# Second mixture-of-experts stage: where squares, high parts, output products and sums stand in a step

## The chip, the cores and the metric

One core of a Trainium2 chip. The metric is device time in microseconds (us) of one execution of the whole program, median of several. TensorE (PE) multiplies matrices, VectorE (DVE), ScalarE (ACT) and GpSimd (POOL) work elementwise, SyncE (SP) issues transfers. Each engine runs its own instructions strictly in the order in which they were issued, and waits on semaphores for the others.

## The reference

Attention over 4 batches of 8 heads and 576 positions with a decaying bias gives 2304 tokens of 512 features. Two expert layers follow, each 512 to 2048 to 512:

```python
def _moe_ref(x, w_in, w_out):
    h = np.maximum(x @ w_in, 0.0)
    return (h * h @ w_out).astype(np.float32)

def _moe2_ref(x, w_in, w_out):
    h = x @ w_in
    g = h * np.cos(h)
    return (g @ w_out).astype(np.float32)
```

## The kernel before, in words

The order is written by hand (a manual schedule): what a function issues first stands first on its engine. Attention and the first layer run woven together; this ends some 624 us into the span, and the second layer runs to the end.

**The second layer** works on five token blocks `j` (four of 512 tokens, the last of 256) and 16 feature slices `f` of 128. `GROUPS` cuts the slices into three passes `p` (4, 5 and 7 slices), and `steps2` is the list of all (p, j, f): 80 steps. In step i,

- `m2_g1` multiplies block j by slice f of the input weights: 12 matmuls on PE into `hp` (three PSUM buffers). Numbers are split into a high and a low half (`yh`, `yl`; two parts per weight), so there are three passes per 128 rows;
- `m2_cos` makes the cosine's argument `a` on ACT, rounds it on DVE in two instructions (`kf`), and takes the sine on ACT;
- `m2_mul` multiplies hp by the cosine on DVE and rounds it to `gh` (on POOL in pass 0, on ACT in passes 1 and 2);
- `m2_rest` makes the low half `gl` of the step before (DVE in passes 0 and 2, POOL in pass 1);
- `m2_g2` multiplies `gh`, `gl` of step i - 2 (`G2LAG`) by the output weights: 12 matmuls into up to four PSUM tiles `o0` to `o3`, one buffer each. After the last slice of a group they are evicted: in pass 0 `o0`, `o2` by ACT and `o1`, `o3` by DVE; later `o0`, `o2` by DVE and the others by ACT with an addition on POOL.

So a full step is 24 matmuls of 512 columns, and the next block's output products cannot start before `o0` is evicted.

**Weights** of the second layer are prepared on the way, a fraction per step (`P_BITS`; `B8_BITS` in the last block of the first layer). Each of 32 weight tiles is clipped by ACT (`w_clip`), gets its bits from DVE (`w_bits`, two instructions) and is squared by ACT with a row sum (`w_square`). `w_sums` adds the rows on PE: a matmul of one column into the PSUM tile `stat`. `w_scales` reads `stat` and computes the scale of a pair of tiles in short DVE instructions (`powers`), and `w_hi` (ACT, 16-bit high part) and `w_lo` (DVE, low part, in `w_lows`) split it. Lists hold the tiles between these stages: `wsq`, `wold`, `wsum`, `wnext`, `wrest`, `wlow`; `w_age` shifts them once a step. `w_step` issues low parts, high parts, bits and squares together, `w_ahead` the clips and loads of later tiles.

**Inputs** of the next block come from DRAM and are scaled by POOL (`yr`), rounded by ACT (`yh`) and subtracted by POOL (`yl`): `split_y`, called by `ready_y` in pass 0. At steps 1 and 5 two parts are issued, so the second `yh` waits for POOL's `yr`.

`step` is the step of attention and of the first layer; its last block prepares weights of the second layer too, with the same functions.

Of the kernel before, what the change touches and what calls it, by code (L numbers as in the profile page):

```python
# [23 lines left out]
NF = DFF // 128  # L24
# [6 lines left out]
GROUPS = ((0, 4), (4, 9), (9, 16))  # L31
RAWS = 6
NB2 = 5
LAG = (3, 5)
G2LAG = 2
# [3 lines left out]
def _weave(*chains):  # L39

    chains = [iter(c) for c in chains if c is not None]
    while chains:
        for c in list(chains):
            if next(c, c) is c:
                chains.remove(c)
# [50 lines left out]

EARLY = 16
FIRST_BITS = 4
B8_BITS = 0.7
P_BITS = 0.6  # L100
CLIP_AHEAD = 2
B0_BITS = 1.5
# [2 lines left out]
XST = 2  # L105
DR_BITS = 1
XST_TO = 20
# [6 lines left out]
def attention_moe_moe_kernel(  # L114
# [211 lines left out]
    lag1, wrest = [], []  # L326
# [357 lines left out]
    nw = [2, 0, 0]  # L684
    stq = [(wp, 3)]
# [55 lines left out]
    def w_square(j):  # L741
        m, f, a = wq[j]
        rw, st = wst[j]
        nc.scalar.activation(
            out=rw.rearrange("p c t -> p (c t)")[:, 0:512].bitcast(F32), in_=st, func=ACTF.Square,
            accum_out=sm["wss"][:, 2 * f + a:2 * f + a + 1],
        )
# [161 lines left out]
    def ready_y(j, i, n):  # L909

        todo = []
        for a in range(blocks[j][1] // BT):
            todo += [lambda a=a, c=c: split_y(j, a, c) for c in range(0, KD, 2)]
        todo += [lambda a=a: load_y(j + 1, a) for a in range(blocks[j + 1][1] // BT if j + 1 < NB2 else 0)]
        for x in range(len(todo) * i // n, len(todo) * (i + 1) // n):
            todo[x]()
# [17 lines left out]
    def moe_slot():  # L934
        part, n = slots.pop(0)
        k, f = chunks[n]
        if part == 1:
            w_need(2 * f + 1)
            g1(k, f)
            return n  # L940
        w_need(2 * f + 2)
        rests(n)
        g2(k, f)
        g2done[0] += 1
        if k == NB1 - 1 and 2 * f >= RAWS:
            w_load(2 * (NF + f))
            w_load(2 * (NF + f) + 1)
            nw[0] = max(nw[0], 2 * (NF + f + 1))
# [20 lines left out]
    def step(moe=0, bits=0, attn=True):  # L969

        i = prog[0]
        prog[0] += attn
        if attn:
            for j in stage(1, i - 2):
                emit_exp(j)
        x_high()
        if attn and job(i - 2):
            emit_turn(i - 2)
        if attn:
            heads_ahead(i, (next_, load_ext, 2))  # L980
        w_age()
        n = moe_slot() if moe else None
        if attn:
            heads_ahead(i, (nhigh, prep_high, 2))
        _weave(evacuate())
        if not attn:
            rests()
        _weave(softmax_tail(i) if attn else None, w_step(bits), v_early())
        x_low()
        rests()  # L990
        w_lows()
        if attn and job(i - 1) and jobs[i - 1][0] < EARLY:
            for j in stage(1, i - 1):
                emit_exp(j)
        act(n)
        if attn:
            heads_ahead(i, (nlow, prep_low, 2))
        if attn and job(i):
            emit_qk(i)
        w_sums()  # L1000
        for _ in range(moe - 1):
            act(moe_slot())
        w_scales()
        if attn:
            for j in stage(1, i - 1):
                emit_exp(j)
        if attn:
            for j in stage(0, i - 2):
                if jobs[j][1] == 0:
                    load_v(jobs[j][0])  # L1010
            for j in stage(3, i - LAG[0]):
                if j > i - lag(j):
                    stages[3] -= 1
                    break
                emit_pv(j)
        turn()
        w_ahead()
        v_late()
        if attn:
            heads_ahead(i, (nraw, load_raw, 4))  # L1020
        if later and prog[0] >= later[0][0]:
            later.pop(0)[1]()
# [6 lines left out]
    def w_clip_to(k):  # L1029
        while nw[1] <= min(k, wlim[0] - 1):  # L1030
            w_load_to(nw[1])
            w_clip(nw[1])
            nw[1] += 1

    def w_rest(j):
        w_hi(j)
        wlow.append(j)

    wlow, wsq, wold, wsum, wnext = [], [], [], [], []

    def w_age():
        wsum.extend(wold)
        wold[:] = wsq
        wsq.clear()

    def w_sums():
        while wsum:
            m, f, a = wq[wsum[0]]
            sum_rows(2 * f + a, (sm["wss"], 2 * f + a))
            wnext.append(wsum.pop(0))  # L1050

    def w_scales():
        while len(wnext) > 1:
            w_scale(wq[wnext[0]][1])
            wrest.extend(wnext[0:2])
            del wnext[0:2]

    def w_lows():
        while wlow:
            w_lo(wlow.pop(0))  # L1060

    def w_step(n):

        js = list(range(nw[2], min(nw[2] + n, wlim[0])))
        while wlow:
            w_lo(wlow.pop(0))
            yield
        while wrest:
            w_rest(wrest.pop(0))
        if js:  # L1070
            w_clip_to(js[-1])
            for _ in zip(*[w_bits(j) for j in js]):
                yield
            for j in js:
                if wq[j][0] == 0:
                    wrest.append(j)
                else:
                    w_square(j)
                    wsq.append(j)
            nw[2] += len(js)  # L1080

    def w_ahead():
        if prog[0] < FIRST_BITS:
            return
        w_clip_to(nw[2] - 1 + min(CLIP_AHEAD, stq[0][1] + (XST if nw[2] + 3 < XST_TO else 0) - len(wrest) - len(wlow) - len(wsq) - len(wold) - len(wsum) - len(wnext)))
        w_load_to(nw[2] - 1 + (WAHEAD if prog[0] else 3))

    def w_stats(j):

        while nw[2] < j:  # L1090
            _weave(w_step(1))
            w_ahead()
        if any(x < j for x in wsq + wold + wsum + wnext):
            w_age()
            w_age()
            w_sums()
            w_scales()
# [17 lines left out]
    while prog[0] < unit_done(0):  # L1115
        i = prog[0]
        x = i - FIRST_BITS
# [77 lines left out]
    hd2 = {}  # L1195
# [17 lines left out]
    def m2_cos(j, f):  # L1213
        n = blocks[j][1]
        hp = hd2[j, f]
        a = p2.tile([128, n], F32, tag="a", bufs=2, name="a")
        kf = p2.tile([128, n], F32, tag="kf", bufs=2, name="kf")
        nc.scalar.activation(out=a, in_=hp, func=ACTF.Copy, scale=sm["hsc"][:, j, f:f + 1], bias=0.25)  # L1218
        nc.vector.tensor_scalar(out=kf, in0=a, scalar1=MAGIC, scalar2=None, op0=ALU.add)  # L1219
        nc.vector.scalar_tensor_tensor(  # L1220
            out=kf, in0=kf, scalar=MAGIC, in1=a, op0=ALU.subtract, op1=ALU.subtract
        )
        nc.scalar.activation(out=a, in_=kf, func=ACTF.Sin, scale=-6.2831850)  # L1223
        hd2[j, f] = (hp, a)

    def m2_mul(p, j, f):
        n = blocks[j][1]
        hp, a = hd2[j, f]
        gh = p2.tile([128, n], F16, tag="gh", bufs=3, name="gh")
        nc.vector.scalar_tensor_tensor(  # L1230
            out=a, in0=hp, scalar=sm["gsc"][:, f:f + 1], in1=a, op0=ALU.mult, op1=ALU.mult
        )
        (nc.scalar.copy if p else nc.gpsimd.tensor_copy)(gh, a)
        hd2[j, f] = (a, gh)

    def m2_rest(p, j, f):
        n = blocks[j][1]
        a, gh = hd2[j, f]
        gl = p2.tile([128, n], F16, tag="gl", bufs=3, name="gl")
        (nc.gpsimd if p == 1 else nc.vector).tensor_tensor(out=gl, in0=a, in1=gh, op=ALU.subtract)  # L1240
        hd2[j, f] = (gh, gl)
# [35 lines left out]
    for i in range(len(steps2) + G2LAG):  # L1277
        new = i < len(steps2)
        w_age()
        if new:  # L1280
            p, j, f = steps2[i]
            w_stats(2 * NF + 2 * GROUPS[p][1])
            w_need(2 * NF + 2 * f + 2)
            m2_g1(j, f)
            m2_cos(j, f)
        w_sums()
        if i == 3:
            y_sums(NB2 - 1, NB2)
        if new and p == 0 and j + 1 < NB2:
            ready_y(j + 1, f, GROUPS[0][1])  # L1290
        if 1 <= i <= len(steps2):
            m2_rest(*steps2[i - 1])
        if new:
            goal = min(4 * NF, bits0 + int((i + 1) * P_BITS))
            _weave(w_step(max(0, goal - nw[2])))
            if nw[2] < 4 * NF:
                w_ahead()
            m2_mul(p, j, f)
            w_lows()
        w_scales()  # L1300
        if i == 4:
            y_scales(NB2 - 1, NB2)
        if i >= G2LAG:
            m2_g2(*steps2[i - G2LAG])


def _lay_out(inputs):
# [44 lines left out]
```

## Time and profile before

| | |
|---|---|
| median of 3 runs | 1031.16 us (1029.96 to 1033.33) |
| the profiled execution | 1031.54 us, of it the span of its instructions 1029.6 us |
| busy in the span | PE 94%, PEld (weight load) 72%, DVE 71%, ACT 63%, POOL 17% |
| 575 to 624 us, end of the first layer | PE 45.13 of 49.00 us, ACT 36.17, DVE 28.90 |
| 624 to 762 us | PE 121.60 of 138.00, DVE 98.85, ACT 77.05, POOL 42.26 |
| 762 to 900 us | PE 134.45 of 138.00, DVE 83.18, ACT 66.99 |
| 900 to 1029.6 us | PE 124.84 of 129.60, DVE 71.41, ACT 51.75 |

The clock numbers are us from the start of the span. Matmuls overlap, so busy PE is not PE at its peak, but idle PE is time lost.

### The profile page before, as it was taken

Reading aid. Unit: us, or ns where it says so; the run is one execution under the profiler, and the core shown is the slowest. Engines: PE = TensorE matmul, PEld = TensorE weight load, DVE = VectorE, ACT = ScalarE, POOL = GpSimd, SP = SyncE. Lnnn points to the kernel's source line nnn. Section 1 sums busy time; section 2 is a strip of 40 time slices with the busy share of each in tenths; the row PEclk is TensorE's granted clock in tenths of the full one; section 3 lists DMA queues with packets and bytes.
Section 4 is the critical chain, followed back from the end, with each engine's and each line's share of the span. In section 5 each row is a group of like instructions: output and inputs, shape, how many; then the busy total and the mean of one; then the engine's idle time right before and its main releaser. Section 6 shows DMA issues by size and latency. Waiting matters only on the chain.

```text
span 1029.6 us, 20440 instructions
## 1 busy us (share of the span) xinstructions
PE 969.4 (94%) x7266; PEld 738.3 (72%) x7266; DVE 727.4 (71%) x1862; ACT 648.7 (63%) x1574; POOL 175.9 (17%) x286
## 2 busy tenths in 40 slices
PE   4999899999999999999999987898899999999998
PEld 3788898899999998999999984344444444444444
DVE  4969889878778887777984366778756665455555
ACT  3879777777777787776764676545555544344433
POOL 4000011111111111111110023443123332011000
PEclk9999999999999999999999999899999999999999
DMA  8945489757888875487894687110000000011001
GB/s 238 332 152 176 120 202 198 169 127 156 178 170 192 181 163 150 120 171 149 204 221 89 232 304 251 42 41 1 1 1 0 1 1 1 1 41 42 11 31 62
DMA packets 150150, 126.65 MB, mean 123 GB/s; under 512 B 108064, under 2 KB 125040, under 8 KB 150048
## 3 DMA queue, kind: packets, MB, share of 16 engines
q1 hardware_dynamic: 145840, 118.20, 44.5%
q0 software_dynamic: 4192, 7.14, 2.9%
q8 instruction: 57, 0.93, 0.4%
q14 instruction: 45, 0.37, 0.1%
q10 hardware_dynamic: 16, 0.01, 0.0%
HBM read 85.25 MB, written 15.81 MB: 98 GB/s over the span
## 4 chain that ended last, share of the span: by engine, by line
PE 67%; DVE 14%; ACT 9%; DMA 5%; issue 3%; POOL 1%; SPq 1%; DVEq 0%; ACTq 0%; POOLq 0%
PE hps L839 17%; PE y L868 16%; PE o L1253 13%; PE hp L1206 11%; PE qkp L491 4%; PE pvs L585 4%; DVE st L711 2%; DVE kf L1220 2%; DVE kf L1219 1%; ACT a L1218 1%; DMA rw<-in_w_dram 1%; ACT a L1223 1%; DVE a L1230 1%; DMA c_d<-one 1%; DMA raw<-in_qk_dram 1%
## 5 line engine op out<-in xcount | busy, mean ns | idle before, releaser
L839 PE MATMUL hps<-xh,wt 128*128 128x256 f32 x1152 | 239.0, 290 | 6.9 <-ACT g L850 6.8
L868 PE MATMUL y<-gh,wt 128*128 128x256 f32 x1152 | 238.0, 290 | 0.0
L839 PEld LDWEIGHTS hps<-xh,wt 128*128 128x128 f32 x1152 | 189.9, 192 | 10.8 <-ACT g L850 9.4
L868 PEld LDWEIGHTS y<-gh,wt 128*128 128x128 f32 x1152 | 189.6, 191 | 1.3
L1206 PE MATMUL hp<-yh,wt 128*128 128x512 f16 (+1 forms) x640 | 186.4, 358 | 0.1
L1253 PE MATMUL o<-wt,gh 128*128 128x512 f16 x576 | 173.8, 384 | 10.3 <-ACT wt L1268 4.9
L868 PE MATMUL y<-gl,wt 128*128 128x256 f32 x576 | 163.1, 283 | 1.6 <-DVE gl L858 1.6
L839 PE MATMUL hps<-xl,wt 128*128 128x256 f32 x576 | 163.2, 283 | 0.9 <-DVE xl L656 0.9
L1206 PEld LDWEIGHTS <-wt 128*128 128x128 f16 x960 | 93.8, 98 | 97.9 <-issue 2.7
L1219 DVE TENSOR_SCALAR kf<-a 128x512 f32<-128x512 f32 (+1 forms) x80 | 37.4, 468 | 118.8 <-ACT a L1218 118.8
L850 ACT ACTIVATE g<-hps 128x256 f32<-128x256 f32 x144 | 54.8, 380 | 105.6 <-PE hps L839 102.4
L1223 ACT ACTIVATE a<-kf 128x512 f32<-128x512 f32 (+1 forms) x80 | 47.0, 587 | 113.9 <-DVE kf L1220 113.9
L1206 PE MATMUL hp<-yl,wt 128*128 128x512 f16 (+1 forms) x320 | 114.5, 358 | 1.5 <-POOL yl L907 1.5
L1253 PE MATMUL o<-wt,gl 128*128 128x512 f16 x288 | 110.4, 383 | 2.5 <-DVE gl L1240 2.5
L868 PEld LDWEIGHTS y<-gl,wt 128*128 128x128 f32 x576 | 110.5, 192 | 2.4 <-DVE gl L858 1.8
L839 PEld LDWEIGHTS hps<-xl,wt 128*128 128x128 f32 x576 | 110.7, 192 | 1.4 <-DVE xl L656 1.1
L1253 PEld LDWEIGHTS <-gh 128*128 128x128 f16 x576 | 55.2, 98 | 74.3 <-issue 14.2
L335 POOL DMA_DIRECT2D k<-ext_d x80 | 41.0, 513 | 331.8 <-ACT g L851 101.4
L522 ACT ACTIVATE sb<-sb,nb 128x128 f32<-128x128 f32 (+8 forms) x160 | 93.7, 586 | 2.9 <-DVE nb L505 2.6
L505 DVE CUSTOM_DVE_ANT_0 sb<-qkp,mask 128x128 f32<-128x128 f32 (+8 forms) x160 | 72.7, 455 | 16.3 <-PE qkp L482 10.9
L858 DVE TENSOR_TENSOR gl<-g,gh 128x256 fp32r<-128x256 f32 x144 | 60.1, 418 | 27.2 <-ACT gh L852 17.6
L1218 ACT ACTIVATE a<-hp,hsc 128x512 f32<-128x512 f32 (+1 forms) x80 | 51.3, 641 | 41.3 <-PE hp L1206 35.7
(115 smaller groups left out, 1691.6 us busy)
## 6 DMA issues: line engine op xcount, KB each, us to landing
rw<-in_w_dram SPq DMA_DIRECT2D x64, 512.0 KB
raw<-in_qk_dram SPq DMA_DIRECT2D x32, 352.0 KB
raw<-in_qk_dram SPq DMA_DIRECT2D x16, 384.0 KB
vr<-in_v_dram POOLq DMA_DIRECT2D x16, 320.0 KB, 4.9
v_d<-vt SPq DMA_DIRECT2D x16, 320.0 KB
raw<-in_qk_dram SPq DMA_DIRECT2D x16, 320.0 KB
vb<-v_d SPq DMA_DIRECT2D x32, 160.0 KB
y_d<-yst SPq DMA_DIRECT2D x18, 256.0 KB
```

The lines of the kernel that those rows point to most:

```text
L491: nc.tensor.matmul(p[0:r, 0:cn], m[0:kk, qo:qo + r], m[0:kk, BT + c0:BT + c0 + cn], start=(kk == 128), stop=(kk == 68),)
L505: nc.vector.tensor_tensor_reduce(out=sb[0:r, c0:c0 + cn], in0=p[0:r, 0:cn], in1=mask[0:r, mo + c0:mo + c0 + cn], scale=-0.125, scalar=(3.0 ...
L522: nc.scalar.activation(out=sb[0:r, 0:w], in_=sb[0:r, 0:w], func=ACTF.Exp, scale=-1.0, bias=j["nb"], accum_out=pd[n - h % 2]["z"][0:r, ti, ...
L839: nc.tensor.matmul(hp, w[:, a, c * 128:(c + 1) * 128], (xh, xl)[e][:, c, :], start=(n == 0), stop=(n == 3 * KD - 1),)
L850: nc.scalar.activation(out=g, in_=hp, func=ACTF.Relu)
L858: nc.vector.tensor_tensor(out=gl, in0=g, in1=gh, op=ALU.subtract)
L868: nc.tensor.matmul(yps[k][d // 2][:, d % 2, :], w[:, a, d * 128:(d + 1) * 128], (gh, gl)[e], start=(f == 0 and n == 0 and d % 2 == 0), sto ...
L1206: nc.tensor.matmul(hp, w[:, a, c * 128:(c + 1) * 128], (yh, yl)[e][:, c, :], start=(m == 0), stop=(m == 3 * KD - 1),)
L1218: nc.scalar.activation(out=a, in_=hp, func=ACTF.Copy, scale=sm["hsc"][:, j, f:f + 1], bias=0.25)
L1219: nc.vector.tensor_scalar(out=kf, in0=a, scalar1=MAGIC, scalar2=None, op0=ALU.add)
L1223: nc.scalar.activation(out=a, in_=kf, func=ACTF.Sin, scale=-6.2831850)
L1253: nc.tensor.matmul(ops[j][a], (gh, gl)[e][:, a * 128:(a + 1) * 128], w[:, x, :], start=(first and m == 0), stop=(last and m == 2),)
```

## The change

Within a step of the second layer, the same instructions are issued in another order. Squares wait in a new list `wbit` and are issued, with all high parts and the `yh` roundings, between the argument and the sine (`m2_cos` is cut, the sine is `m2_sin`). Low halves and the output products with their evictions come next; low parts, bits and the multiplication follow them. `w_scales` moves to the start of a step, `w_sums` to its end (after the output products on PE), and `wold` goes. In the first layer's last block `w_scales` and `w_sums` move the same way, and squares are issued one `w_step` later. `B8_BITS` 0.75 prepares ten weight tiles there instead of nine.

```diff
-B8_BITS = 0.7
+B8_BITS = 0.75
@@ step
         w_age()
+        w_scales()
         n = moe_slot() if moe else None
...
-        w_sums()
         for _ in range(moe - 1):
             act(moe_slot())
-        w_scales()
+        w_sums()
@@
     def w_age():
-        wsum.extend(wold)
-        wold[:] = wsq
+        wsum.extend(wsq)
         wsq.clear()
+
+    def w_squares():
+        while wbit:
+            w_square(wbit[0])
+            wsq.append(wbit.pop(0))
@@ w_step
             yield
+        w_squares()
         while wrest:
             w_rest(wrest.pop(0))
...
                 else:
-                    w_square(j)
-                    wsq.append(j)
+                    wbit.append(j)
@@ the loop over steps2
         w_age()
+        w_scales()
+        if i == 5:
+            y_scales(NB2 - 1, NB2)
         if new:
             p, j, f = steps2[i]
             w_stats(2 * NF + 2 * GROUPS[p][1])
             w_need(2 * NF + 2 * f + 2)
             m2_g1(j, f)
             m2_cos(j, f)
+            w_squares()
+            while wrest:
+                w_rest(wrest.pop(0))
+            if p == 0 and j + 1 < NB2:
+                ready_y(j + 1, f, GROUPS[0][1])
+            m2_sin(j, f)
+        if 1 <= i <= len(steps2):
+            m2_rest(*steps2[i - 1])
+        if i >= G2LAG:
+            m2_g2(*steps2[i - G2LAG])
+        if new:
+            w_lows()
+            goal = min(4 * NF, bits0 + int((i + 1) * P_BITS))
+            _weave(w_step(max(0, goal - nw[2])))
+            m2_mul(p, j, f)
+            if nw[2] < 4 * NF:
+                w_ahead()
         w_sums()
         if i == 3:
             y_sums(NB2 - 1, NB2)
-        if new and p == 0 and j + 1 < NB2:
-            ready_y(j + 1, f, GROUPS[0][1])
-        if 1 <= i <= len(steps2):
-            m2_rest(*steps2[i - 1])
-        if new:
-            goal = min(4 * NF, bits0 + int((i + 1) * P_BITS))
-            _weave(w_step(max(0, goal - nw[2])))
-            if nw[2] < 4 * NF:
-                w_ahead()
-            m2_mul(p, j, f)
-            w_lows()
-        w_scales()
-        if i == 4:
-            y_scales(NB2 - 1, NB2)
-        if i >= G2LAG:
-            m2_g2(*steps2[i - G2LAG])
```

ACT in step 5, where block 0 is evicted for the first time (argument, sine, `yh`, clips, evictions, next argument), before:

```order
L1218 ACTIVATE a<-hp_10478,hsc 128x512
L1223 ACTIVATE a<-kf 128x512
L906 CAST yh<-yr 128x2x256 x2
L701 ACTIVATE st<-rw 128x512 x2
L1268 ACTIVATE wt_9805<-o_10357,osc 128x512
L1268 ACTIVATE wt_9936<-o_10359,osc 128x512
L1218 ACTIVATE a<-hp_10528,hsc 128x512
```

and of the change:

```order
L1222 ACTIVATE a<-hp_10485,hsc 128x512
L744 ACTIVATE rw,wss<-st 128x512
L906 CAST yh<-yr 128x2x256 x2
L1231 ACTIVATE a<-kf 128x512
L1276 ACTIVATE wt_9805<-o_10365,osc 128x512
L1276 ACTIVATE wt_9939<-o_10367,osc 128x512
L1222 ACTIVATE a<-hp_10535,hsc 128x512
```

A square and both `yh` now stand ahead of the sine, and no clip ahead of the evictions.

DVE in the step of pass 1 that evicts block 0 (kf rounds the argument, L1230 is the multiplication, L760 to L765 are scales, L1260 evicts), before:

```order
L1219 TENSOR_SCALAR kf<-a 128x512
L1220 SCALAR_TENSOR_TENSOR kf<-kf,a 128x512
L707 TENSOR_SCALAR st<-st 128x512
L711 SCALAR_TENSOR_TENSOR st<-rw,st 128x512
L1230 SCALAR_TENSOR_TENSOR a<-hp_11419,gsc,a 128x512
L760 TENSOR_SCALAR wsm<-stat 128x2
L761 TENSOR_SCALAR wex<-wsm 128x2
L765 TENSOR_SCALAR wsc<-wex 128x2
L1260 SCALAR_TENSOR_TENSOR wt_9805<-o_11274,osc,wt_9805 128x512
L1260 SCALAR_TENSOR_TENSOR wt_9936<-o_11276,osc,wt_9936 128x512
```

and of the change, where the multiplication is L1238 and the eviction L1268:

```order
L760 TENSOR_SCALAR wsm<-stat 128x2
L761 TENSOR_SCALAR wex<-wsm 128x2
L765 TENSOR_SCALAR wsc<-wex 128x2
L1223 TENSOR_SCALAR kf<-a 128x512
L1224 SCALAR_TENSOR_TENSOR kf<-kf,a 128x512
L1268 SCALAR_TENSOR_TENSOR wt_9805<-o_11282,osc,wt_9805 128x512
L1268 SCALAR_TENSOR_TENSOR wt_9939<-o_11284,osc,wt_9939 128x512
L735 SCALAR_TENSOR_TENSOR wt_11444<-st,wsc,wt_11444 128x512
L735 SCALAR_TENSOR_TENSOR wt_11446<-st,wsc,wt_11446 128x512
L707 TENSOR_SCALAR st<-st 128x512
L711 SCALAR_TENSOR_TENSOR st<-rw,st 128x512
L1238 SCALAR_TENSOR_TENSOR a<-hp_11426,gsc,a 128x512
```

The evictions passed the multiplication; two low parts (L735), which stood behind it, stand ahead of it.

PE in step 5 where the input products (hp) end, before:

```order
L1206 MATMUL hp_10478<-yh,wt_9936 128x512
L753 LDWEIGHTS onesb
L753 MATMUL stat<-wss,onesb 128x1
L1253 LDWEIGHTS gh
L1253 MATMUL o_10357<-wt_10208,gh 128x512
```

and of the change at the end of that step's output products:

```order
L1261 MATMUL o_10368<-wt_10169,gl 128x512
L753 LDWEIGHTS onesb
L753 MATMUL stat<-wss,onesb 128x1
L1210 LDWEIGHTS wt_10029
L1210 MATMUL hp_10535<-yh,wt_10029 128x512
```

The sum into `stat` moved behind the twelve output products.

## Rows read from the trace of the kernel before

**Rows 1.** Who PE waited for, 575 to 624 us: total us, times, longest.

```profile
PE hps L839 <- ACT g L850: 3.7, 6, 1.1
```

**Rows 2.** Who PE waited for, 624 to 900 us: total us, times, longest.

```profile
PE o L1253 <- ACT wt L1268: 4.9, 2, 2.5
PE stat L753 <- DVE wsm L760: 4.6, 2, 3.3
PE o L1253 <- DVE wt L1260: 3.5, 3, 1.9
PE o L1253 <- DVE gl L1240: 1.6, 1, 1.6
PE o L1253 <- DVE wt L1270: 1.6, 2, 1.3
PE hp L1206 <- POOL yl L907: 1.5, 2, 1.0
PE stat L753 <- DVE ysm L760: 1.2, 1, 1.2
PE stat L753 <- ACT rw L744: 0.8, 1, 0.8
```

**Rows 3.** All engines, 640 to 680 us: window, length, busy, PEclk, DMA.

```profile
640.00:680.00 40.00, 33.75 (x144) 14.34 (x143) 28.96 (x54) 21.01 (x40) 16.14 (x16) 0.91 0.15 47
```

**Rows 4.** The chain that ended last, 570 to 900 us: start, us, what.

```profile
640.30 2.14 DVE wt L735 x2
...
660.38 1.16 POOL yl L907
661.54 1.11 POOL yr L902
...
665.02 4.42 PE o L1253 x12
...
672.04 2.59 PE o L1253 x12
```

**Rows 5.** Groups on ACT, 575 to 900 us: busy us, mean ns, idle before and releaser.

```profile
L1218 ACT ACTIVATE a<-hp,hsc 128x512 f32<-128x512 f32 (+1 forms) x54 | 35.0, 647 | 24.9 <-PE hp L1206 19.3 <-PE stat L753 5.5
L1223 ACT ACTIVATE a<-kf 128x512 f32<-128x512 f32 (+1 forms) x53 | 31.5, 594 | 77.9 <-DVE kf L1220 77.9
L726 ACT ACTIVATE wt<-st,wsc 128x512 f16<-128x512 f32 x32 | 21.2, 709 | 0.0
L744 ACT ACTIVATE rw<-st 128x512 f32<-128x512 f32 x32 | 20.0, 626 | 17.5 <-DVE st L711 17.5
L701 ACT ACTIVATE st<-rw 128x512 f32<-128x512 f32 x32 | 19.7, 659 | 0.3 <-DMA yr<-y_d 0.3
L1233 ACT CAST gh<-a 128x512 f16<-128x512 f32 (+1 forms) x33 | 19.2, 581 | 15.4 <-DVE a L1230 15.4
L906 ACT CAST yh<-yr 128x512 f16<-128x512 f32 x18 | 10.9, 607 | 5.0 <-POOL yr L902 5.0
L744 ACT ACTIVATION_READ_ACCUMULATOR rw<-st 128x1 f32 x32 | 6.0, 186 | 0.0
```

**Rows 6.** Groups on DVE, 624 to 762 us, columns as above.

```profile
L1230 DVE SCALAR_TENSOR_TENSOR a<-hp,gsc,a 128x512 f32<-128x512 f32 (+1 forms) x25 | 17.6, 705 | 4.4 <-ACT a L1223 4.4
L735 DVE SCALAR_TENSOR_TENSOR wt<-st,wsc,wt 128x512 f16<-128x512 f32 x17 | 14.9, 911 | 2.9 <-ACT wt L726 2.8
L711 DVE SCALAR_TENSOR_TENSOR st<-rw,st 128x512 int32<-128x512 int32 x16 | 11.1, 693 | 0.5
L707 DVE TENSOR_SCALAR st<-st 128x512 int32<-128x512 int32 x16 | 6.7, 420 | 0.0
```

**Rows 7.** Single instructions in order of time: start, us, engine, instruction, idle before.

```profile
623.51 0.74 DVE L735 SCALAR_TENSOR_TENSOR wt<-st,wsc,wt 128x512 f16<-128x512 f32 x1
...
623.62 0.63 ACT L744 ACTIVATE rw<-st 128x512 f32<-128x512 f32 x1 [1.40 <-DVE st L711]
...
635.86 0.39 PE L1253 MATMUL o<-wt,gl 128*128 128x512 f16 x1
```

More of the change, by code (lines that the diff above doesn't have):

```diff
@@ L1037, in w_rest @@
         wlow.append(j)
-    wlow, wsq, wold, wsum, wnext = [], [], [], [], []
+    wlow, wbit, wsq, wsum, wnext = [], [], [], [], []
     def w_age():
-        wsum.extend(wold)
-        wold[:] = wsq
+        wsum.extend(wsq)
         wsq.clear()
+    def w_squares():
+        while wbit:
+            w_square(wbit[0])
+            wsq.append(wbit.pop(0))
     def w_sums():
@@ L1084, in w_ahead @@
             return
-        w_clip_to(nw[2] - 1 + min(CLIP_AHEAD, stq[0][1] + (XST if nw[2] + 3 < XST_TO else 0) - len(wrest) - len(wlow) - len(wsq) - len(wold) - len(wsum) - len(wnext)))
+        w_clip_to(nw[2] - 1 + min(CLIP_AHEAD, stq[0][1] + (XST if nw[2] + 3 < XST_TO else 0) - len(wrest) - len(wlow) - len(wbit) - len(wsq) - len(wsum) - len(wnext)))
         w_load_to(nw[2] - 1 + (WAHEAD if prog[0] else 3))
@@ L1092, in w_stats @@
             w_ahead()
-        if any(x < j for x in wsq + wold + wsum + wnext):
-            w_age()
+        if any(x < j for x in wbit + wsq + wsum + wnext):
+            w_squares()
             w_age()
@@ L1222, in m2_cos, with m2_sin @@
         )
+        hd2[j, f] = (hp, a, kf)
+    def m2_sin(j, f):
+        hp, a, kf = hd2[j, f]
         nc.scalar.activation(out=a, in_=kf, func=ACTF.Sin, scale=-6.2831850)
@@ L1285, in attention_moe_moe_kernel @@
             m2_cos(j, f)
+            w_squares()
+            while wrest:
[14 more added lines that the diff above has]
+                w_ahead()
         w_sums()
```

## Prediction

> **What bounds the kernel now.** I read the shares first: PE is busy 94% of the span, so time can only come from PE's idle time or its clock. Then the stretches (table above): only those between 575 and 900 us, where the change acts, have idle PE worth naming, so I asked there whom PE waits for. At the end of the first layer it is ACT alone, 3.7 us in six waits for `g` [rows 1]. In the second layer it is a list of 14 waits with eight names, together 19.7 us [rows 2]: evicted output tiles (ACT 4.9, DVE 3.5 and 1.6), the tile `stat` still to be read (4.6 and 1.2) or its square still to be made (0.8), a low half `gl` (1.6), an input low half `yl` (1.5). The reader should see that each is an instruction late behind other work on its engine, not an engine that is full. Third, the clock: between 640 and 680 us the granted clock averages 0.91 [rows 3], in rows at either 2.4 or 1.2 GHz, after the long waits there; 9% of 40 us is 3.6 us. The chain shows one of the two stretches: twelve output matmuls in 4.42 us, which take 2.59 at full clock a step later [rows 4], 1.8 us lost. In all 27.0 us could be had.
>
> Last the groups of ACT: its sine waits 77.9 us for the rounding on DVE in 53 instructions, 1.47 us each, and its squares wait 17.5 us for the bits that DVE makes in the same step [rows 5]. What is put into the first wait costs ACT nothing up to 1.47 us.
>
> **The change part by part.** All work stays (one weight tile is prepared a little earlier); I count only waits. One step of full size is 2 x 2.59 = 5.18 us of PE [rows 4].
>
> *End of the first layer.* The square is issued a step later, so ACT no longer stands before it (17.5 us over the whole stretch; one such wait is the 1.40 us at 623.62, [rows 7]) while the next `g` queues behind. ACT works 36.2 us in these 49 (table above) and gets one tile more (clip 0.66, square 0.63 + 0.19, high part 0.71: 2.2 us, [rows 5]): 38.4 of some 45 us, 85%, in order. I leave 1.0 of 3.7 us: +2.7 (0 to 3.7).
>
> *Start of the second layer.* PE's first three input products run ahead, and the first output product needs `gl` of step 0, now at 635.86 [rows 7]. ACT's first argument comes 1.4 us earlier (the wait gone). Between it and the sine stand a square 0.81, two high parts 1.42 and a `yh` 0.61, 2.84 us in a hole of 1.47: 1.4 us back. Two clips (1.32) instead of one `yh` precede the second argument, 0.7 later; DVE's scales no longer stand ahead of its rounding, which gives about as much. I take 635.86 unchanged: the 3.3 us at `stat` [rows 2] go, but PE idles as long for `gl`: 0 (-2 to +3.3). One step later the sine's delay is over and arguments come early again: the waits for the square (0.8), `gl` (1.6) and the half clock behind them (1.8) go: +4.2.
>
> *Sums at step ends, scales at step starts.* A sum now has the twelve output products between its square and itself and finds `stat` read long ago. The 1.2 for `ysm` goes: +1.2. Queued behind a sum is the next input product, which would stop if the read were late; the scales wait for nothing but that sum and stand first on DVE, so I see no new wait.
>
> *First eviction, step 5.* Count from the end of the input product: argument 0.65, square 0.81, `yh` 0.61, then POOL's `yl` 1.16 and `yr` 1.11 [rows 4] for which the second `yh` 0.61 waits, sine 0.59 [rows 5], eviction some 0.65 (like ACT's groups of this size): 6.2 us. PE returns to the tile after 5.18. So about 1.2 us with latencies remain of 2.5 [rows 2]: +1.3; and a wait so short need not lower the clock: +1.8 (0 to 1.8).
>
> *Input low halves.* `yh` stands ahead of the sine, 1.47 + 0.59 = 2.1 us earlier, more than the longest wait for `yl` (1.0): +1.3 of 1.5.
>
> *Other evictions.* In pass 1 DVE evicts right after its rounding, 2 us after the input product, when the tiles are ready, not behind bits, multiplication, low parts and scales: 3.5 us, all gone: +3.5 (2 to 3.5). DVE's other evictions (1.6 in pass 0) likewise, and `wsm` at the border to pass 1 (4.6 - 3.3 = 1.3) and ACT's second late eviction (2.4): 5.3 us. But the four short steps of block 4 give PE 2.6 us each and DVE still the weights of a long one, so DVE arrives late whatever the order. I leave 2.0: +3.3 (0 to 5.3).
>
> *What it costs.* A step with a pair of high parts becomes longer: low parts wait for them and the multiplication waits for both. On ACT: 0.65 + 0.81 + 1.42 = 2.9 us to the second high part, the low parts (0.91 each, [rows 6], one beginning earlier) to 4.0, bits (0.42 + 0.69) to 5.1, multiplication 0.71 to 5.8; with low parts both behind, 6.5. In pass 0 the next rounding is free then and `gl` is ready at 8.4 us or so, while PE wants it at 10.4. In pass 1 the rounding `gh` (0.58) is on ACT too and the next argument stands behind it: 6.4 to 7.1 us against 5.18. Before, the low parts lay behind the multiplication and the same loop was 0.65 + 1.47 + 0.59 + 1.42 + 0.81 + 0.58 = 5.5. Pass 1 has four such steps of some 13; the light ones take 0.65 + 1.47 + 0.59 + 0.71 + 0.58 = 4.0 and bring it back. The mean is near PE's 5.18, so I charge 2.0: -2.0 (0 to 4 x 1.9 = 7.6).
>
> The low parts' price has two ends. Alone, one takes 0.74 us [rows 7]; where POOL is at work in between, a pair took 2.14 [rows 4]. The earlier `yh` starts POOL's `yl` just when low parts run, in the four steps of pass 0 that have both.
> The Trainium skill ("SBUF — State Buffer", section "SBUF: two separate sides") says that VectorE with two SBUF inputs and a GpSimd instruction that reads SBUF take a shared port in turn, the second blocked until the first is done. The 2.14 us agree. By that rule the four pairs would take about 1.2 us more each; by the rows alone 0.66 more at most.
> Either way it is DVE time in steps with 2 us to spare, and counts only in the second rival.
>
> **Sum.** 2.7 + 4.2 + 1.2 + 3.1 + 1.3 + 3.5 + 3.3 - 2.0 = 17.3 us. The profiled execution took 1031.5 us, its span 1029.6 and 1.9 around it, which stay; 1031.5 - 17.3 = 1014.2. The median lies 0.4 below the profiled execution, so I forecast 1014 us.
>
> **The rivals.**
> *Half of it is given back* (1020 to 1028, about 1023). The longer steps cost in pass 0 too, or block 4 and the border to pass 1 keep all of 5.3 us, and the clock falls again at the start: 2.0 more for block 4, 3.6 for the clock, 3 to 4 for the steps make 9. For it: DVE is busy 99 of 138 us from 624 to 762 (table above), and the second `yh` makes ACT wait for POOL (5.0 us, [rows 5]) now ahead of a sine. Against: the slack of 2 us in pass 0.
> *The multiplication behind the low parts decides: slower.* Some ten pairs of tiles are left for the second layer (20 of 32 tiles). If the loop from argument to argument holds PE in each, 7.1 - 5.18 = 1.9 us, that is 19 us, as much as the gains (19.3), and with 2 us more at the start and two stretches of half clock (3.6) the time is 1037. It decides from 1.9 us a pair on. For it: in pass 1 the loop passes ACT twice. Against: six of the ten pairs fall into pass 0, where POOL makes `gh`.
> *The waits only move* (1028 to 1034, no change): each tile evicted earlier makes PE wait for `gl` instead, since `gl` is bound by the same chain. Against: the step at 672.04 [rows 4], with the same chain and no eviction, runs its products in 2.59 us without a wait.
> *All of it* (1004 to 1009): start, first eviction and border free as well, and no longer steps: 8 us more.
>
> **Chances.** Forecast (1009 to 1020) 0.60; half given back 0.18; all of it 0.08; the waits move 0.06; slower 0.08. A measurement of this kernel tells some 0.3%, 3.1 us, from no change: faster 0.60 + 0.18 + 0.08 = 0.86, same 0.06, slower 0.08. The range 1005 to 1026 holds the forecast, three quarters of the best case and most of the half case, about 0.81.
>
> **What would show it.** Right: PE waits no longer for `wsm`, `ysm` and `wt L1260`; the sine's wait for `kf` shrinks from 77.9 us to under 50 and the squares' wait from 17.5 to under 3; one PE wait of 3 to 5 us for `gl` remains at the first output product, one of about 1 us at the first eviction; the clock is 1.0 but for one stretch at most. Wrong: waits for `gl` or `gh` all through pass 0 and pass 1; waits for `hp`'s argument on DVE's `a`; a wait for ACT's `o` evictions as long as now; PE waiting for ACT's `g` as before at the end of the first layer.

## The result

| | before | after |
|---|---|---|
| median (lowest to highest), 4 runs each | 1032.24 us (1029.96 to 1036.26) | 1017.69 us (1013.93 to 1020.06) |
| profiled execution, its span | 1031.54, 1029.6 us | 1016.88, 1015.1 us |

The ratio is 0.9852, 95% interval 0.9807 to 0.9896. The change makes the kernel faster by about 14.5 us; 17.3 had been forecast. One further run of the kernel before took 1585.04 us at a granted clock of 0.571 and is left out of all comparisons.

Where PE waited in the changed kernel, first from 575 to 624 us, then from 624 to 900 us (who for whom: total us, times, longest):

```profile
PE hps L839 <- ACT g L850: 0.9, 1, 0.9
```

```profile
PE o L1261 <- ACT wt L1276: 2.5, 2, 1.5
PE o L1261 <- DVE gl L1248: 2.3, 1, 2.3
PE o L1261 <- ACT a L1231: 1.7, 1, 1.7
PE o L1261 <- POOL gh L1241: 1.4, 1, 1.4
PE o L1261 <- DVE wt L1268: 1.1, 2, 0.6
PE o L1261 <- POOL gl L1248: 0.7, 2, 0.5
PE hp L1210 <- POOL yl L907: 0.2, 1, 0.2
```

The first row answers to [rows 1]: 3.7 us have become 0.9. The others answer to [rows 2]: 19.7 us (19.9 with one wait of 0.2 for `gh` that is not in those rows) have become 9.9, and nothing waits for `stat` or the square any more. The row that names `a` L1231 is an eviction too: ACT's `os` behind a late sine, at 787 us.

The groups on ACT from 575 to 886 us show why (columns as in [rows 5]). The sine waits 47.3 us for the rounding instead of 77.9, and the squares wait for nothing instead of 17.5. The price is in the last row: `yh`, which now stands ahead of a sine, waits 13.7 us for POOL's `yr` instead of 5.0.

```profile
L1231 ACT ACTIVATE a<-kf 128x512 f32<-128x512 f32 (+1 forms) x53 | 31.4, 592 | 47.3 <-DVE kf L1224 47.2
...
L744 ACT ACTIVATE rw<-st 128x512 f32<-128x512 f32 x32 | 19.9, 622 | 0.0
...
L906 ACT CAST yh<-yr 128x512 f16<-128x512 f32 x18 | 11.0, 612 | 13.7 <-POOL yr L902 13.7
```

The granted clock, by windows (columns as in [rows 3]): the half clock is not gone but lies earlier, in one stretch behind the first output product's waits.

```profile
624.00:632.00 8.00, 6.17 (x30) 2.47 (x28) 4.21 (x8) 7.13 (x12) 2.19 (x3) 1.00 0.87 341
632.00:640.00 8.00, 6.11 (x16) 2.28 (x17) 7.18 (x12) 4.36 (x9) 4.94 (x5) 0.57 0.20 67
640.00:680.00 40.00, 38.54 (x185) 17.48 (x183) 35.08 (x59) 22.73 (x43) 17.42 (x17) 1.00 0.13 42
```

To see where the time came from I cut the second layer at three PE instructions that every variant has: its first input product, the input product of step 7, and the first output product of pass 1. The last part ends with the span.

| us | first product at | to step 7 | rest of pass 0 | passes 1 and 2 |
|---|---|---|---|---|
| before | 624.06 | 45.22 | 78.28 | 282.04 |
| after | 621.59 | 39.69 | 72.05 | 281.77 |
| forecast gain | 2.7 | 4.2 + 1.2 + 3.1 = 8.5 | 1.3 + 3.3 = 4.6 | 3.5 - 2.0 = 1.5 |
| measured gain | 2.47 | 5.53 | 6.23 | 0.27 |

The parts are those of one profiled run and hold its half clock: up to step 7 the granted clock averaged 0.92 before and 0.91 after.

### The profile page after: what moved, and what is told of

Read it like the earlier page. It is cut to its first block, busy times and chain, and to the rows that moved or that the text cites. A ratio compares the mean times of both kernels' runs of the same rounds, so it can differ in the third digit from the quotient of the medians.

```text
span 1015.1 us, 20449 instructions
## 1 busy us (share of the span) xinstructions
PE 967.2 (95%) x7266; PEld 738.4 (73%) x7266; DVE 732.6 (72%) x1862; ACT 647.7 (64%) x1574; POOL 178.0 (18%) x286
## 4 chain that ended last, share of the span: by engine, by line
PE 68%; DVE 14%; ACT 7%; DMA 4%; issue 4%; POOL 1%; SPq 1%; DVEq 0%; ACTq 0%; POOLq 0%
PE hps L839 18%; PE y L868 17%; PE o L1261 11%; PE hp L1210 11%; PE qkp L491 4%; PE pvs L585 4%; DMA early<-in_qk_dram 3%; DVE a L1238 2%; DVE kf L1223 2%; ACT a L1222 2%; DVE wt L735 1%; DVE kf L1224 1%; DMA rw<-in_w_dram 1%; DVE st L711 1%; ACT st L701 1%
## 5 line engine op out<-in xcount | busy, mean ns | idle before, releaser
L1223 DVE TENSOR_SCALAR kf<-a 128x512 f32<-128x512 f32 (+1 forms) x80 | 41.2, 515 | 106.3 <-ACT a L1222 106.3
L1231 ACT ACTIVATE a<-kf 128x512 f32<-128x512 f32 (+1 forms) x80 | 46.9, 586 | 79.4 <-DVE kf L1224 79.4
L554 DVE SCALAR_TENSOR_TENSOR p<-sb,p 128x512 f16<-128x512 f32 (+7 forms) x128 | 72.4, 565 | 4.1 <-DVE p L550 0.2
```

Of the source, the lines that this page charges most:

```text
L554: nc.vector.scalar_tensor_tensor(out=p[0:r, cw:cw + w], in0=sb[0:r, 0:w], scalar=PSC, in1=p[0:r, 0:w], op0=ALU.mult, op1=ALU.subtract,)
```

## The experiments

All times together first. Each run of a kernel also has a mean granted clock, and the runs of one and the same program follow it: the changed kernel took 1013.93, 1016.88, 1018.50 and 1020.06 us at 1.000, 0.995, 0.992 and 0.991. Over the 123 runs of all kernels, each kernel around its own mean, a thousandth of clock is worth 0.75 us (least squares). The last column moves each run to clock 1.000 by that and takes the median; it is an estimate, good to about 1 us at best.

| kernel | median us (runs) | ratio to before, 95% | to step 7 / rest of pass 0 / passes 1, 2 | at clock 1.000 |
|---|---|---|---|---|
| before | 1032.27 (49) | | 45.22 / 78.28 / 282.04 | 1027.8 |
| after | 1017.69 (4) | 0.981 to 0.990 | 39.69 / 72.05 / 281.77 | 1013.2 |
| e5 number alone | 1029.55 (12) | 0.995 to 0.999 | 43.24 / 77.09 / 282.09 | 1025.1 |
| e2 first layer, number | 1027.17 (8) | 0.993 to 0.997 | 45.57 / 77.30 / 282.33 | 1022.7 |
| e3 = e2 + evictions ahead | 1026.90 (6) | 0.992 to 0.996 | 47.34 / 76.65 / 280.37 | 1021.1 |
| e4 = e2 + squares ahead | 1017.81 (5) | 0.983 to 0.987 | 38.30 / 75.47 / 280.38 | 1015.5 |
| e1 = after, old number | 1021.94 (6) | 0.987 to 0.991 | 40.76 / 75.42 / 284.04 | 1019.1 |
| e8 = after, squares behind | 1022.59 (6) | 0.988 to 0.993 | 41.04 / 76.49 / 282.71 | 1020.5 |
| e6 = after, `yh` late | 1017.12 (4) | 0.982 to 0.987 | 36.16 / 76.95 / 281.79 | 1015.2 |
| e7 = after, low parts late | 1017.85 (4) | 0.983 to 0.988 | 40.82 / 74.74 / 279.51 | 1014.7 |
| e9 = e7 in pass 1 on only | 1014.33 (5) | 0.982 to 0.987 | 38.16 / 72.03 / 279.52 | 1011.2 |
| e10 = e6 in some steps | 1014.64 (4) | 0.981 to 0.985 | 37.83 / 72.05 / 281.66 | 1013.9 |
| e11 = e9 and e10 | 1012.09 (4) | 0.979 to 0.982 | 37.83 / 72.04 / 279.50 | 1010.6 |
| e12 = e11, other steps | 1010.90 (6) | 0.977 to 0.983 | 36.15 / 73.21 / 279.58 | 1010.0 |

The changed kernel's four runs give it a wide interval, which those of all kernels but e2, e3 and e5 overlap. Every run of e1 and e8 is slower than its slowest; smaller differences from it rest on the parts and on the last column. In the parts, the clock up to step 7 averaged 0.92 in e5, 0.89 in e2, 0.90 in e3, 0.96 in e4 and 1.00 in e6, e9, e10 and e11.

**Theory and rivals.** My theory was the prediction's sum: each part of the change removes the waits that were put down to it. The rivals: one part does nearly all; the number of tiles prepared early, costed at nothing, does part of it; the places of `yh` and of the low parts give some of it back.

**The first layer and the number.** Undone in the changed kernel, and set alone in the kernel before:

```diff
-B8_BITS = 0.75      # e1, in the changed kernel
+B8_BITS = 0.7
-B8_BITS = 0.7       # e5, in the kernel before
+B8_BITS = 0.75
```

> The changed kernel with B8_BITS back at 0.7, so that one tile fewer is prepared in the first layer. My theory: the 2.5 us gained at the end of the first layer come from the squares issued a step later, not from this number, so the second layer still starts at 621 to 622.5 us with PE's waits from 575 to 624 us at 1 us or less, and the time stays within 1 us of the changed kernel's (the tile is prepared in the second layer instead, one step with a pair more, up to 2 us). Rival (the number decides there): the waits for g come back, 3 us or more, and the second layer starts near 624.

> The kernel before with B8_BITS at 0.75 alone. Theory A (the number is worth its 4 us by itself, by one tile less in a second layer that is late at its start): 1027 to 1030 us, 3 to 6 us under before. Theory B (it pays only where squares no longer hold ACT, since the end of the first layer gets a tile more): no change or up to 2 us slower, with PE's waits for g at the end of the first layer at 3.7 us or more.

At the end of the first layer PE waited for `g` 0.9 us in e1, as in the changed kernel, and in e5 somewhat longer than in [rows 1]:

```profile
PE hps L839 <- ACT g L850: 4.6, 8, 1.1
```

So the 2.8 us there come from the new order in the first layer, and the number has no part in them. That it is the squares issued later, as forecast, fits ACT's wait for the bits, which is gone; the sums and scales that moved with them were not tried apart. But e1 is 4.2 us slower than the changed kernel, 5.9 at equal clock: my "within 1 us" falls, and so does theory B for e5, which gained 2.7. The number works in the second layer. One tile more is done when it begins, and each pair of high parts falls into another step; no run with a third number tells what the one is worth and what the other. In e1 one pair falls into the step that makes the last `yh` of a block; two rows of the timeline and the one that waits (start, us, engine, instruction, idle before):

```profile
687.80 1.33 ACT L726 ACTIVATE wt<-st,wsc 128x512 f16<-128x512 f32 x2 [1.01 <-DVE wsc L765]
...
689.04 0.60 ACT L906 CAST yh<-yr 128x512 f16<-128x512 f32 x1
...
689.72 1.38 POOL L907 TENSOR_TENSOR yl<-yr,yh 128x512 f16<-128x512 f32 x1 [1.98 <-ACT yh L906]
...
691.15 0.38 PE L1210 MATMUL hp<-yl,wt 128*128 128x512 f16 x1 [1.08 <-POOL yl L907]
```

The high parts wait 1.01 us for their scale and hold `yh`, and PE stops for `yl`. In the changed kernel that step has no high parts: `yh` comes right behind the argument, at 686.16, and PE doesn't stop. e1 waits another 1.4 us for `yl` near 713 us, where a square stands ahead of `yh` and the high parts a step earlier, and 4.0 us for `stat` at the start.

**One part alone in the second layer.** e2 has the loop in its old order (with `B8_BITS` 0.75, the new first layer, squares a step after their bits); e3 and e4 add one part each:

```diff
         if 1 <= i <= len(steps2):
             m2_rest(*steps2[i - 1])
+        if i >= G2LAG:                       # e3: from the step's end
+            m2_g2(*steps2[i - G2LAG])
...
             m2_cos(j, f)
+            w_squares()                      # e4
+            while wrest:
+                w_rest(wrest.pop(0))
             m2_sin(j, f)
```

> The second layer's loop in its old order (squares before the next bits, no longer behind them in the same step; scales also at the first step); the first layer as changed. My theory: the second layer starts near 621.6, 2.5 us earlier than before, and the waits for wt and o evictions (11 of 20 us) and most of the start stay as before; the squares' wait for bits goes, which lets the argument start earlier and the wait for stat shrink from 4.6 to under 3. In all 1025 to 1029 us, 3 to 6 us under the kernel before. Rival (the deferred square alone does the work in the second layer too): below 1021.

> As the run with the old order of the second layer, with the output products and evictions alone moved ahead of bits, multiplication and low parts. My theory: the DVE evictions' waits (wt 3.5 us, o 1.6) go for the most part and ACT's become shorter, so 4 to 7 us less than that run, 1019 to 1023. Rival (an eviction is late because its sine or the square ahead of it is late): less than 2 us of difference and the waits for wt as long as before.

> As the run with the old order of the second layer, with squares and high parts alone moved between argument and sine. My theory: 2 to 4 us less than that run, 1023 to 1026, by the waits for the square and stat and the gl behind them; the waits for wt and o stay at 8 us or more. Rival (this is the part that matters): within 2 us of the changed kernel.

e2's time is as expected, its waits are not: PE's waits at `stat` were to shrink, and are 9.3 us (below) against 6.6 in [rows 2], most of them for the square that now comes a step later. e3 gained 0.3 us where 4 to 7 were expected (1.6 at equal clock), and e4 gained 9.4 where 2 to 4 were (7.2 at equal clock): its median is the changed kernel's. Part of that mends what e2's mixture of late squares and early sums made worse, since e4 waits 0.5 us at `stat`. In e4 the waits for `wt` were still 5.9 us, and still the gain was there. What e3 did is seen in PE's waits from 618 to 900 us, e2 first:

```profile
PE stat L753 <- ACT rw L744: 7.7, 3, 5.0
PE o L1261 <- ACT wt L1276: 3.7, 3, 2.8
PE stat L753 <- DVE wt L1278: 1.6, 1, 1.6
...
PE o L1261 <- DVE wt L1268: 1.3, 2, 0.8
```

```profile
PE stat L753 <- ACT rw L744: 14.2, 7, 5.4
...
PE o L1261 <- ACT wt L1276: 1.1, 1, 1.1
...
PE o L1261 <- DVE wt L1268: 0.6, 1, 0.6
```

The evictions' waits went as forecast, 5.0 to 1.7 us in these two names. But the square on ACT now stood behind the evictions as well, and a sum on PE that stands early in a step waited 6.5 us more for it. For this part alone "the waits only move" was right, though they moved to `stat` and not to `gl` as that rival had it.

**Squares taken out of the whole.** The counterpart:

```diff
             m2_cos(j, f)
-            w_squares()
-            while wrest:
-                w_rest(wrest.pop(0))
             if p == 0 and j + 1 < NB2:
```

> The changed kernel with squares and high parts issued behind the evictions again, with the next bits, and all else as changed (yh ahead of the sine, output products and evictions ahead, sums at step ends). If squares and high parts between argument and sine carry the gain in the second layer, 8 to 10 us are lost: 1025 to 1028 us, with PE's waits for the square or stat back at 3 us or more at the start. If the evictions' place or the sums' place carries it, 1018 to 1021.

1022.59: 4.9 us lost (7.3 at equal clock), between the two expectations. PE's waits from 621 to 900 us:

```profile
PE o L1261 <- ACT wt L1276: 3.6, 2, 2.5
...
PE stat L753 <- ACT rw L744: 2.0, 1, 2.0
```

Do the parts add? From e2's 1027.2 to the changed kernel's 1017.7 it is 9.5 us. Squares and high parts alone (e4) give 9.4 of them, all the other parts without them (e8) give 4.6: by the medians the parts do not add. At equal clock they give 7.2 and 2.2 of 9.5, and they do add. These runs do not decide it. Either way squares and high parts are the larger part. In e8 PE waits 2.0 us at `stat` where e2 waits 9.3, with the sums at the step's end; so the two ways out of that wait, earlier squares and later sums, overlap.

**The low parts.** e7 puts them behind the multiplication in all steps; e9, run after it, from pass 1 on:

```diff
-            w_lows()
+            low = []
+            if p:                 # e9; e7 without this condition
+                low, wlow[:] = wlow[:], []
+            w_lows()
             goal = min(4 * NF, bits0 + int((i + 1) * P_BITS))
             _weave(w_step(max(0, goal - nw[2])))
             m2_mul(p, j, f)
+            wlow[:] = low + wlow
+            w_lows()
```

> The changed kernel with the low parts behind the multiplication (bits, multiplication, low parts). By my sum the low parts ahead of the multiplication cost 2.0 us (0 to 7.6) in pass 1: 1014 to 1016, and the waits in pass 1 (1.7 for the eviction behind a late argument, 0.5 twice for gl) go. Rival (DVE stands at the multiplication till the sine is done, and the low parts then delay the next rounding): 1 to 5 us slower, with waits for gh or gl in pass 0.

> The changed kernel with the low parts behind the multiplication in pass 1 alone. The price of low parts ahead of the multiplication in pass 1, by the last pair of traces, is some 2 us (the second layer lost nothing in pass 1 with them behind): from the first product of pass 1 to the end 2 us less than the changed kernel, the wait of 1.7 us at the eviction near 787 us gone; the start as in the changed kernel. 1015 to 1016.5 us. If DVE's order is not what makes it late, the wait stays.

1014 to 1016 us had been expected of e7. Its median is the changed kernel's, but its parts are not. Passes 1 and 2 took 2.26 us less, and the wait at 787 us was gone: the 2.0 that the prediction charged. Pass 0 took 3.8 us more. At its start DVE stood 3.13 us at the multiplication till the sine was done (with a table load of 1.28 us ahead of it on ACT), and the low parts came after; the second argument, and `gl` behind it, were late:

```profile
628.08 0.75 DVE L1238 SCALAR_TENSOR_TENSOR a<-hp,gsc,a 128x512 f32<-128x512 f32 x1 [3.13 <-ACT a L1231]
628.75 1.76 DVE L735 SCALAR_TENSOR_TENSOR wt<-st,wsc,wt 128x512 f16<-128x512 f32 x2
...
634.63 0.61 PE L1261 MATMUL o<-wt,gl 128*128 128x512 f16 x1 [4.01 <-DVE gl L1248]
```

So low parts ahead of the multiplication pay in pass 0 and cost in pass 1, where ACT rounds `gh` too. e9 kept the first and took back the second: 279.52 us for passes 1 and 2, 3.4 us less by the medians, 2.0 at equal clock. The runs of the two kernels overlap, but those passes do not: 279.50 to 279.58 us in the four kernels with the low parts late there (e7, e9, e11, e12), 281.66 to 281.79 in the three that differ in the place of `yh` at most (the changed kernel, e6, e10).

**The input halves.** In the changed kernel the first late eviction, in step 5, reads like this (rows as above):

```profile
655.30 1.55 POOL L902 TENSOR_SCALAR yr<-yr,ysc 128x1024 f32<-128x1024 f32 x1
...
656.89 0.62 ACT L906 CAST yh<-yr 128x512 f16<-128x512 f32 x1 [3.05 <-POOL yr L902]
657.41 0.62 ACT L1231 ACTIVATE a<-kf 128x512 f32<-128x512 f32 x1
...
657.94 1.24 ACT L1276 ACTIVATE wt<-o,osc 128x512 f32<-128x512 f32 x2
...
658.66 0.59 PE L1261 MATMUL o<-wt,gh 128*128 128x512 f16 x2 [1.46 <-ACT wt L1276]
```

The second `yh` of that step waits for POOL, and the sine and the eviction wait behind it. e6 puts `ready_y` behind the evictions in all steps, e10 in the steps of the first block and the first step (f == 0) of the others; e11 is e9 and e10 together; e12 takes f == 1, since it is the second step of a block, not the first, that evicts the block before and has two `yh`:

```diff
+            late = j == 0 or f == 0        # e12: f == 1
-            if p == 0 and j + 1 < NB2:
+            if p == 0 and j + 1 < NB2 and not late:
                 ready_y(j + 1, f, GROUPS[0][1])
...
         if i >= G2LAG:
             m2_g2(*steps2[i - G2LAG])
         if new:
+            if p == 0 and j + 1 < NB2 and late:
+                ready_y(j + 1, f, GROUPS[0][1])
             w_lows()
```

> The changed kernel with the input halves yh (and POOL's yl behind them) moved from ahead of the sine to behind the output products and evictions. If yh ahead of the sine is what leaves waits at the first eviction (1.5 us for the pass-0 eviction in step 5, 1.0 in the last step of the second block's), these fall under 0.5, and the subtraction gl at the start, 1.64 us beside POOL's yl, takes 0.7 again, so that the wait of 2.3 for it falls under 1.3: 2 to 4 us gained, less 1 to 1.3 of waits for yl that come back: 1015 to 1017. Rival (the place of yh decides nothing): within 0.5 us in every one of these waits.

> The changed kernel with the input halves behind the evictions only in the steps of the first block and in the first step of each later block; in the other steps ahead of the sine. Expected: the start as with all of them late (no stretch at half clock from 632 to 639 us, 3 to 4 us less up to the step behind the first eviction), without the waits for yh and yl near 687 and 711 us (2.5 and 1.2 us): 1013 to 1015 us. If the place of yh at the start is not the cause of the half clock, 1017 again.

> Both of these edits: 1011 to 1014 us, 4 to 6 us under the changed kernel, if their gains (3 to 4 at the start, 2 in pass 1) lie in different stretches and add; 1015 or more if the second takes back what the first gives.

> As the run with both edits, with the input halves behind the evictions in the second step of each block of pass 0 instead of the first: that is the step in which the tiles of the block before are evicted, and the one with POOL's yr between the two yh. If yh ahead of the sine there is what holds up the evictions, the waits of 1.5 us near 655 and of 1.0 us near 698 go: 1009 to 1011 us, 1.5 to 2.5 us under that run. If the evictions are late for another reason, both waits stay; if the input halves then come too late, PE waits for yl instead, 1 us or more near 687 or 711 us.

e6 took 1017.12 us where 1015 to 1017 had been expected. The start took 36.16 us instead of 39.69, without the eviction's wait; but it ran at full clock, and e9, at full clock too, took 38.16, so that 2.0 us are the order's. The rest of pass 0 took 4.9 more, 3.2 of it in waits near 687 and 711 us, and by estimate 1.7 in the lower clock behind the first (0.95 from 675 to 690 us, 0.90 from 690 to 700):

```profile
PE hp L1210 <- POOL yl L907: 2.0, 2, 1.1
...
PE hp L1210 <- ACT yh L906: 1.2, 1, 1.2
```

In e12 both waits for ACT's evictions are gone, which settles their cause: in e11, with f == 0, they were 1.5 and 1.0, as in the changed kernel:

```profile
PE o L1261 <- ACT wt L1276: 2.5, 2, 1.5
```

The list of PE's waits from 620 to 900 us in e12 begins:

```profile
PE o L1261 <- DVE gl L1248: 2.3, 2, 1.3
PE o L1261 <- POOL gh L1241: 1.7, 1, 1.7
PE o L1261 <- DVE wt L1268: 1.1, 2, 0.6
PE hp L1210 <- POOL yl L907: 1.1, 2, 0.9
```

In their place stand 1.25 us for `gl` at 664.75 and 0.89 for `yl` at 690.28, so that little is left of the gain: 0.6 us against e11 at equal clock. e12 and e11 are the fastest kernels here, 2.0% under before; at equal clock most of what they gain on the changed kernel is e9's edit (2.0 of 2.6 and 3.2 us).

**The clock at the start.** e10 was to show that `yh` behind the evictions keeps the half clock away there, and its trace and e11's have none. But e9 starts in the order of the changed kernel, with the same waits, 1.43 for `gh` and 2.28 for `gl`, and has none either (the same stretch as above, its layer beginning 2 us earlier):

```profile
630.00:638.00 8.00, 5.71 (x26) 2.47 (x27) 7.18 (x12) 4.37 (x9) 4.95 (x5) 1.00 0.19 68
```

And e12, with the short waits of e11, has it again: 0.79 in its 632 to 640. So one and the same order runs with and without. The changed kernel itself has a run at 1.000 (1013.93 us), where a stretch like that of its profiled run would leave 0.997 (estimate: 8 us at 0.57 in 1015). At equal clock e10 is worth nothing (1013.9 against 1013.2). What lowers the clock in one run and not in another stays open.

## Why the prediction was right, and where not

*End of the first layer.* Right in place and size: PE's waits went from 3.7 to 0.9 us by the new order there (e1, e5), of which the squares were not tried alone. The 2.47 us of the table prove less than the waits: kernels with one and the same first layer began the second anywhere from 617.80 us (e2) to 624.16 (e12), at a clock of 1.00 and 0.99 over the first 575 us.

*"All work stays (one weight tile is prepared a little earlier)": charged at nothing but ACT's 2.2 us.* This step failed. The number is worth 2.7 us alone and 4.2 in the changed kernel. I had costed the tile's work and not asked what one tile less, and pairs in other steps, do to the second layer. It also means that the closeness of the forecast is in part luck: e1, which has every part that the sum counted and not the number, took 1021.94 us, a gain of 10.3 instead of 17.3, and outside the forecast's 1009 to 1020.

*Start of the second layer (+4.2) and first eviction (+3.1).* With the +1.2 for sums, 8.5 forecast and 5.53 found. The sums' waits went as said. The clock's 3.6 us did not come in the profiled run, whose half clock lies in one stretch instead of two; e9, with none, gained 7.06 here by the same order. The 1.4 us missing in e9 are two sizes. The first eviction, by the chain that was forecast, kept more than 1.2 us: 1.46 in the changed kernel, and in e9

```profile
655.13 0.59 PE L1261 MATMUL o<-wt,gh 128*128 128x512 f16 x2 [2.11 <-ACT wt L1276]
```

The other is the first product with `gl`. I had taken it unchanged at 11.80 us after the layer's start; it came at 12.30 (12.29 in e9), behind waits of 1.43 for `gh` and 2.28 for `gl` (one wait of 3 to 5 for `gl` had been forecast):

```profile
631.67 1.61 POOL L907 TENSOR_TENSOR yl<-yr,yh 128x512 f16<-128x512 f32 x1 [0.73 <-ACT yh L906]
632.19 1.64 DVE L1248 TENSOR_TENSOR gl<-a,gh 128x512 f16<-128x512 f32 x1
...
633.89 0.61 PE L1261 MATMUL o<-wt,gl 128*128 128x512 f16 x1 [2.28 <-DVE gl L1248]
```

DVE's `gl` begins while POOL's `yl` runs and ends 0.55 us after it: 1.64 us instead of 0.68. Of 44 such `gl` none took that long before, and five do after, since `yh` stands earlier and sends POOL into them. In e11, where `yh` of the first block stands late, this `gl` begins as long after the layer's start (10.61 us; 10.60 in the changed kernel) but meets no `yl`:

```profile
630.04 0.68 DVE L1248 TENSOR_TENSOR gl<-a,gh 128x512 f16<-128x512 f32 x1
...
630.78 0.39 PE L1261 MATMUL o<-wt,gl 128*128 128x512 f16 x1 [1.08 <-DVE gl L1248]
```

Its product comes at 11.35 us, 0.95 earlier. The prediction named this contention for the low parts and let it count only in a rival; here it is 1 us on PE's path. The Trainium skill ("SBUF — State Buffer", section "SBUF: two separate sides") says that a VectorE instruction with two SBUF inputs and a GpSimd instruction that reads SBUF exclude each other until the first is done; the changed kernel's rows agree, with 1.09 us blocked and 0.55 of work after.

*Input low halves (+1.3) and the border (+3.3).* 6.23 found for 4.6: at the border nothing was left of the long wait for ACT, where I had left 2.0 in all; 1.0 remains at 701.54, the second eviction behind a `yh`.

*Evictions of pass 1 (+3.5).* The waits for DVE did fall, 3.5 to 1.1, but not shown by the order that I named: with evictions at the end of the step e4 has 1.5, and e5 1.3 by the number alone (618 to 900 us):

```profile
PE o L1261 <- DVE wt L1268: 1.5, 3, 0.8
```

```profile
PE o L1253 <- DVE wt L1260: 1.3, 2, 0.8
```

For the evictions' order the runs show no gain that can be told.

*The cost of low parts (-2.0).* Right: 2.26 and 2.25 us in passes 1 and 2 (e7, e9), the wait at 787 us with it. The rival that made the kernel slower by it had the sign wrong for pass 0, where low parts ahead of the multiplication save 3.8 us.

In sum the mechanism held (instructions late behind others on their engine, not full engines), with the gain of one edit ascribed to another: squares and high parts carry most of the second layer's gain, the number 2.7 us or more, and evictions next to none by themselves.

## What to carry to other kernels

When an engine executes in order, put what is ready into its known wait, here squares and high parts into the 1.5 us between argument and sine, but not what itself waits for another engine, such as the second `yh`. Whether the parts of a reordering add is not known beforehand: do each alone and undo each in the whole before a gain is ascribed, and compare at equal clock, since here the answer changed with it. A number that sets how far ahead work is done also decides with which steps it coincides; here it was worth 2.7 us alone and 4.2 in the whole, though how much of that is coincidence was not tried.

## What the hardware showed unexpectedly

Runs of one and the same program differ by up to 6 us with the clock they are granted (1013.93 us at 1.000, 1020.06 at 0.991), and equal waits of 1.43 and 2.28 us were followed by half clock in one trace and full clock in another; for effects under 3 us the clock of each run has to be read beside its time. The first sine is preceded by a table load of 1.28 us on ACT, before and after (627.48 us in the changed kernel), ahead of the first output product; moving it was not tried.
